# One spectrum for both filter products, a second inverse table, and a reordered start in a Fourier filter with a dense layer behind it

## The chip, the cores and the metric

The kernel runs on one core of a Trainium2 chip. The metric is the device time of one execution in microseconds (us), median of several executions. An execution whose time lies over 1.5% above the fastest of the same kernel is called slow and is left out of every comparison.

## The reference, cut to what matters

```python
def _attn_ref(x, filt_r, filt_i):          # x: 8 x 3008 x 256
    X = np.fft.rfft(x, axis=1)
    F = (filt_r + 1j * filt_i)[None, :, :]
    return np.fft.irfft(X * F, n=x.shape[1], axis=1)

def _moe_ref(x, w_in, w_out):              # 24064 tokens, 256 -> 2048 -> 256
    h = x @ w_in
    return (0.5 * h * (1.0 + erf(h / sqrt(2)))) @ w_out
```

Each of eight batches is filtered in the frequency domain, and the result goes through two dense layers with a Gelu between them.

## The kernel before

The transform of length 3008 is split into 47 x 64. Its four matmul stages are a first transform by table T1, a second by T2, an inverse by T3 and an inverse by T4. Batches 1 to 7 are filtered in slots between the dense matmuls of the batch before. Batch 0 has no dense work to hide behind: it is filtered alone at the start, in the functions named c1 to c4, while the tables are still being made and the filters and weights are still being loaded. The change concerns only this start and three slot numbers.

The stages of batch 0 (cuts are marked with `# ...`):

```python
def dup_filters(self, eng, k0, k):       # rows 0-63 of the filter table to rows 64-127
    for k in range(k0, k0 + k, 2):
        o, i = (self.F[r:r + 64, :, k:k + 2, :].rearrange("p t a b -> p t (a b)") for r in (64, 0))
        eng.tensor_copy(out=o, in_=i)

def c2(self, p):                         # second transform, then the filter product
    w = self.st[0, "p", p] = self.pp.tile([128, 2, 512], BF16, tag="p12", name="p12")
    ps = self.bank("ps_c2", "w")         # two banks: spectrum and i times spectrum
    for t, o in ((0, 1), (1, 0)):
        for i in range(2):
            k = 2 * p + i
            nc.tensor.matmul(ps[:, t, 256 * i:256 * i + 256],
                             lhsT=self.T2[:, k, o:o + 2].rearrange("p a b -> p (a b)"),
                             rhs=self.st[0, "b", k // 4][:, k % 4, :], start=True, stop=True)
    f = self.F[:, :, 2 * p:2 * p + 2, :]
    if p < 11:
        nc.vector.tensor_tensor(out=w, in0=ps, in1=f.rearrange("p t a b -> p t (a b)"), op=ALU.mult)
        return
    # ...

def c3(self, p, np=2):                   # third transform: two separate banks, two evictions
    # ...
    ps = [self.bank("ps_c3", "n") for half in range(2)]
    # ... matmuls with self.T3 for both products ...
    for half in range(2):
        # ...
        self._evac(v[:, :, 8 * p:8 * p + 8 * np], ps[half][:, 0:256 * np].rearrange("c (k n) -> c n k", n=HB),
                   False if p == 11 and half else "act")

def warm_up(self, n):                    # matmuls on a tile of ones, their result is not used
    ps = self.bank("ps_warm", "w")
    for i in range(n):
        self.nc.tensor.matmul(ps[:, i % 2], lhsT=self.ones[:, 0:128], rhs=self.ones, start=True, stop=True)
```

And the order of the start:

```python
m.psum(wide, w=(2, 2), n=(4, 1))         # 2 buffers of 2 banks, 4 of one bank
# ... iotas, first input part, m.warm_up(10), tables, m.load_x(0, 1, 4) ...
for k, n in ((0, 4), (4, 4), (8, 8), (16, 8)):
    m.load_filters(k, n)
m.dup_filters(nc.gpsimd, 4, 4)
m.load_w_in()
m.dup_filters(nc.gpsimd, 8, 8)
for u in range(16):                      # first transform, 4 matmuls and one eviction per u
    m.c1(u // 2, u % 2, act if u < 4 or u % 2 else False)
    if u == 3:
        m.warm_up(3)
        m.table_2_sin(0)
    if u == 7:
        m.table_2_swap(0)
        m.table_2_minus()
        m.warm_up(3)
        m.table_2_sin(1)
    if u == 11:
        m.warm_up(2)
nc.scalar.activation(out=warm, in_=m.p, func=AF.Gelu)
m.warm_up(2)
m.c1t(0, False)
m.c1t(1, act)
m.dup_filters(nc.vector, 0, 4)
# ...
m.dup_filters(nc.gpsimd, 16, 8)
# ... second batch's input, w_out, then c2 and c3 of 12 pairs of frequencies, then c3t and c4
```

## Time and profile before

| | before |
|---|---|
| median time (3 runs) | 773.84 us (773.63 to 774.07) |
| span of the profiled execution | 772.2 us, mean granted clock 1.000 |
| first filter product starts | 16.72 us |
| last filter product ends | 32.02 us |
| first transpose behind it | 32.99 us |
| dense work starts | 40.55 us |
| first matmul of the second layer | 50.92 us |

In the timeline each line has the start, the length, the engine, the source line and the operation with its count, then in brackets the idle time before it and what ended it. The timeline of TensorE, kernel before:

```profile
6.04 1.44 PE L361 MATMUL ps_c<-T1c,x_sb 94*128 94x96 bf16 x16
7.28 0.84 PE L239 MATMUL ps_warm<-ones 128*128 128x512 bf16 x3
9.38 0.84 PE L361 MATMUL ps_c<-T1c,x_sb 94*128 94x96 bf16 x16 [1.25 <-DMA x_sb<-in_x_dram]
```

Sixteen matmuls of the first transform take 1.44 us at 6.04 and 0.84 us at 9.38. Their number and shape are fixed, so this length is a clock that can be read at any place where they stand. In this execution TensorE came to full speed at about 7.3.

### The profile page before, as it was taken

Reading aid. Unit: us, or ns where it says so; the run is one execution under the profiler, and the core shown is the slowest. Engines: PE = TensorE matmul, PEld = TensorE weight load, DVE = VectorE, ACT = ScalarE, POOL = GpSimd, SP = SyncE. Lnnn points to the kernel's source line nnn. Section 1 sums busy time; section 2 is a strip of 40 time slices with the busy share of each in tenths; the row PEclk is TensorE's granted clock in tenths of the full one; section 3 lists DMA queues with packets and bytes.
Section 4 is the critical chain, followed back from the end, with each engine's and each line's share of the span. In section 5 each row is a group of like instructions: output and inputs, shape, how many; then the busy total and the mean of one; then the engine's idle time right before and its main releaser. Section 6 shows DMA issues by size and latency. Waiting matters only on the chain.

```text
span 772.2 us, 15059 instructions
## 1 busy us (share of the span) xinstructions
PE 763.2 (99%) x6066; PEld 528.7 (68%) x6066; DVE 397.3 (51%) x722; ACT 567.4 (73%) x981; POOL 64.9 (8%) x160
## 2 busy tenths in 40 slices
PE   8999999999999999999999999999999999999998
PEld 4847675676776766677777776666776776766666
DVE  7866755464555645457463664637646366411011
ACT  6879955897568975699656996579865798666663
POOL 7801100020000200011000110001100000000000
PEclk9999999999999999999999999999999999999999
DMA  8894745466253661636516464255553422410111
GB/s 138 145 180 124 150 123 129 128 124 151 57 139 107 138 159 41 192 78 122 143 53 181 85 133 123 79 154 95 124 137 81 139 83 69 123 42 28 42 42 55
DMA packets 87398, 85.66 MB, mean 111 GB/s; under 512 B 6752, under 2 KB 77536, under 8 KB 87328
## 3 DMA queue, kind: packets, MB, share of 16 engines
q1 hardware_dynamic: 78816, 68.70, 31.0%
q0 software_dynamic: 8512, 16.00, 14.9%
q8 instruction: 47, 0.77, 0.4%
q14 instruction: 23, 0.19, 0.1%
HBM read 54.00 MB, written 46.66 MB: 130 GB/s over the span
## 4 chain that ended last, share of the span: by engine, by line
PE 94%; DMA 3%; POOL 2%; issue 0%; DVE 0%; POOLq 0%
PE ps_o L488 43%; PE ps_h L461 42%; PE ps_s L345 2%; PE ps_s L320 2%; PE ps_s L295 2%; PE ps_s L272 2%; DMA x_sb<-in_x_dram 2%; POOL F L96 1%; POOL x_sb L82 1%; DMA F<-in_filt_i_dram 1%; POOL F L91 0%; PE ps_e L478 0%; POOL T1s L258 0%; DVE ost L501 0%; POOL T1p L580 0%
## 5 line engine op out<-in xcount | busy, mean ns | idle before, releaser
L464 ACT ACTIVATE g_sb<-ps_h 128x512 bf16<-128x512 f32 x752 | 438.0, 597 | 182.8 <-PE ps_h L461 172.1
L488 PE MATMUL ps_o<-w_out_sb,g_sb 128*128 128x256 bf16 x2992 | 447.5, 273 | 0.0
L461 PE MATMUL ps_h<-y_sb,w_in_sb 128*128 128x512 bf16 (+3 forms) x1600 | 445.8, 366 | 0.7 <-DMA x_sb<-in_x_dram 0.7
L488 PEld LDWEIGHTS <-g_sb 128*128 128x128 bf16 x2992 | 283.9, 98 | 134.3 <-issue 9.9
L461 PEld LDWEIGHTS <-w_in_sb 128*128 128x128 bf16 x1600 | 154.7, 98 | 23.7 <-issue 1.1
L494 DVE COPY ost<-ps_o 128x512 f32<-128x512 f32 x93 | 63.8, 686 | 143.5 <-PE ps_o L488 143.4
L303 DVE TENSOR_TENSOR p<-ps_s,F 128x512 bf16<-128x512 f32 x84 | 58.1, 691 | 105.9 <-ACT p L302 89.5
L249 DVE TENSOR_SCALAR y_sb<-ps_s 128x376 bf16<-128x376 f32 x112 | 60.9, 548 | 80.5 <-PE ps_s L345 80.5
L247 DVE CAST a_sb<-ps_s 128x512 bf16<-128x512 f32 x112 | 69.3, 682 | 27.7 <-PE ps_s L272 27.7
L247 DVE CAST v_sb<-ps_s 128x512 bf16<-128x512 f32 x84 | 57.4, 684 | 2.9 <-PE ps_s L320 2.6
L301 ACT ACTIVATE p<-ps_s 64x512 bf16<-64x512 f32 x84 | 49.9, 594 | 2.1
L302 ACT CAST p<-ps_s 64x512 bf16<-64x512 f32 x84 | 48.5, 577 | 1.0
L345 PEld LDWEIGHTS <-d_sb 96*128 96x128 bf16 x448 | 30.8, 97 | 25.3 <-DMA d_sb<-R 0.2
L101 POOL COPY gate<-p 1x1 bf16<-1x1 bf16 x48 | 8.5, 178 | 470.3 <-DVE p L305 470.3
L305 DVE TENSOR_TENSOR p<-p 128x512 bf16<-128x512 bf16 x84 | 35.7, 425 | 2.9
L345 PE MATMUL ps_s<-T,d_sb 96*128 96x94 bf16 x448 | 36.3, 204 | 0.0
L304 DVE TENSOR_TENSOR p<-p,F 128x512 bf16<-128x512 bf16 x84 | 34.8, 415 | 0.0
L82 POOL DMA_DIRECT2D x_sb<-in_x_dram x64 | 32.7, 512 | 13.0 <-issue 12.5
L320 PE MATMUL ps_s<-p,T 128*128 128x256 bf16 x168 | 32.1, 273 | 0.0
L295 PE MATMUL ps_s<-b_sb,T 128*128 128x256 bf16 x168 | 32.1, 273 | 0.0
L320 PEld LDWEIGHTS <-T 128*128 128x128 bf16 x168 | 16.4, 98 | 20.1 <-DVE p L305 0.5
L295 PEld LDWEIGHTS <-T 128*128 128x128 bf16 x168 | 16.4, 98 | 13.4
(103 smaller groups left out, 189.1 us busy)
## 6 DMA issues: line engine op xcount, KB each, us to landing
out_dram<-ost SPq DMA_DIRECT2D x93, 256.0 KB, 2.3
x_sb<-in_x_dram POOLq DMA_DIRECT2D x64, 188.0 KB, 3.8
R<-a_sb SPq DMA_DIRECT2D x112, 96.0 KB, 2.1
b_sb<-R SPq DMA_DIRECT2D x28, 384.0 KB, 4.3
R<-v_sb SPq DMA_DIRECT2D x42, 256.0 KB, 3.5
d_sb<-R SPq DMA_DIRECT2D x56, 192.0 KB, 4.7
w_in_sb<-in_moe_w_in_dram POOLq DMA_DIRECT2D x2, 512.0 KB, 7.8
w_out_sb<-in_moe_w_out_dram POOLq DMA_DIRECT2D x2, 512.0 KB, 11.3
```

The costliest lines, as they stand in the source:

```text
L247: self.nc.vector.tensor_copy(out=out, in_=in_)
L249: self.nc.vector.tensor_scalar(out=out, in0=in_, scalar1=scale, scalar2=None, op0=ALU.mult)
L295: nc.tensor.matmul(ps[:, 256 * i:256 * i + 256], lhsT=self.T2[:, k, 1:3].rearrange("p a b -> p (a b)"), rhs=self.st[b, "b", k // 6][:, k % ...
L301: nc.scalar.activation(out=p2[0:64], in_=ps[64:128], func=AF.Copy, scale=-1.0)
L302: nc.scalar.copy(out=p2[64:128], in_=ps[0:64])
L303: nc.vector.tensor_tensor(out=p1, in0=ps, in1=f(0), op=ALU.mult)
L320: nc.tensor.matmul(ps[:, 256 * i:256 * i + 256], lhsT=self.T3[:, k].rearrange("p a b -> p (a b)"), rhs=w[:, 256 * i:256 * i + 256], start= ...
L345: nc.tensor.matmul(ps[:, 94 * i:94 * i + 94], lhsT=d[:, (grp % 2) * 4 + i, 128 * half:128 * half + 128], rhs=t4, start=True, stop=True)
L461: nc.tensor.matmul(ps[:, o:o + n], lhsT=self.w_in_sb[:, dc, jc * 128:jc * 128 + 128], rhs=self.ring[:, dc, off:off + n], start=(dc == 0), ...
L464: nc.scalar.activation(out=self.st["g", t][:, jc, :], in_=ps, func=AF.Gelu)
L488: nc.tensor.matmul(ps[:, tile_i % 2, :], lhsT=g[:, jc, tile_i * 128:tile_i * 128 + 128], rhs=self.w_out_sb[:, jc, :], start=(jc == 0), sto ...
L494: nc.vector.tensor_copy(out=ost, in_=ps)
```

## The change

The intent is to spare work in batch 0. The second spectrum (i times the first) is not computed: the imaginary filter multiplies the same spectrum, and the i moves into a second inverse table, T3i, made from T3 by swapping its two columns with a sign. The third transform gets one buffer of two banks (z) and one eviction in place of two. Angles are reduced by an integer shift in place of two float operations. Most filter rows are copied to the upper half of the table by DMA, four copies stay on Pool and one on VectorE. The input is issued earlier, its last part in halves, and the load of the Gelu table moves from the start to the end of the stage. The core of the diff, cuts marked:

```diff
+    def dup_filters_dma(self, k0, k):
+        self.nc.sync.dma_start(out=self.F[64:128, :, k0:k0 + k, :], in_=self.F[0:64, :, k0:k0 + k, :])
 # ... table_2_angle:
-        v.tensor_scalar(out=r, in0=w, scalar1=RND, scalar2=-RND, op0=ALU.add, op1=ALU.add)
-        v.tensor_tensor(out=w, in0=w, in1=r, op=ALU.subtract)
+        ts(out=self.gen[:, 1, k].bitcast(I32), in0=w[:, k].bitcast(I32), scalar1=15, scalar2=None,
+           op0=ALU.logical_shift_left)
+    def table_3_turn(self, q):
+        k = slice(8 * q, 8 * q + 8)
+        for r in range(2):
+            self.nc.vector.tensor_scalar(out=self.T3i[:, k, r, :], in0=self.T3[:, k, 1 - r, :],
+                                         scalar1=self.turn[r], scalar2=None, op0=ALU.mult)
 # ... c2: one spectrum, read twice
-            nc.vector.tensor_tensor(out=w, in0=ps, in1=f.rearrange("p t a b -> p t (a b)"), op=ALU.mult)
+            nc.vector.tensor_tensor(out=w, in0=ps.unsqueeze(1).to_broadcast([128, 2, 512]),
+                                    in1=f.rearrange("p t a b -> p t (a b)"), op=ALU.mult)
 # ... c3: one buffer of two banks, one eviction
-        ps = [self.bank("ps_c3", "n") for half in range(2)]
+        ps = self.bank("ps_c3", "z")
-                                              rhs=self.T3[:, 2 * (p + i) + k].rearrange("p a b -> p (a b)"),
+                                              rhs=(self.T3i if t else self.T3)[:, 2 * (p + i) + k].rearrange("p a b -> p (a b)"),
 # ... the order
-    m.psum(wide, w=(2, 2), n=(4, 1))
+    m.psum(wide, w=(2, 1), n=(4, 1), z=(1, 2))
-    m.warm_up(10)
+    m.warm_up(9)
+    m.dup_filters_dma(2, 2)
+    m.dup_filters_dma(4, 4)
+    m.dup_filters_dma(16, 8)
+    m.table_2_sin(0)
+    for u in range(16):
+        if u == 4:
+            m.table_2_swap(0)
+            m.table_2_angle(g, 1)
+        if u == 8:
+            m.turn_signs(g)
+            m.weights_4(g)
+            m.table_2_sin(1)
+            m.table_2_swap(1)
+        if u == 12:
+            m.table_4(m.T4c, m.T1q, m.wtc)
+        if u in (4, 8, 12):
+            m.warm_up(2)
+        m.c1(u // 2, u % 2, False if u in (1, 3, 5, 7, 8, 9, 12, 14) else act)
 # ... two of three parts of T3i by table_3_turn, the last one by ScalarE
-            s1, n1, r1, s2, n2, r2, s4, n4 = 1, 4, 16, 26, 2.8, 61, 68, 0.72
+            s1, n1, r1, s2, n2, r2, s4, n4 = 0, 4, 15, 25, 2.8, 61, 68, 0.72
```

The matmuls on ones, here called fillers, go from 10 + 3 + 3 + 2 + 2 = 20 to 9 + 2 + 2 + 2 + 1 = 16 (the last one is in a line that the cut leaves out), and they stand at other places.

## The prediction

> **What bounds the kernel now.** I read the page's list of engines first, then its chain that ended last, then the busy time of each engine in seven stretches, and at last the timeline of the first 41 us.
>
> The stretches, each with its length, then the busy us (and count) of PE, PEld, DVE, ACT, POOL, then granted clock, DMA share and GB/s:
>
> ```profile
> 0.00:6.00 6.00, 4.45 (x10) 1.31 (x10) 3.54 (x25) 1.84 (x3) 4.99 (x21) 1.00 0.56 80
> 6.00:14.50 8.50, 6.61 (x76) 4.34 (x76) 7.93 (x15) 6.59 (x14) 5.64 (x11) 1.00 1.02 180
> 14.50:17.00 2.50, 2.13 (x28) 1.92 (x29) 1.75 (x4) 2.48 (x4) 2.50 (x5) 1.00 1.07 148
> 17.00:28.00 11.00, 10.38 (x139) 9.13 (x137) 10.01 (x9) 10.25 (x17) 10.80 (x14) 1.00 1.00 164
> 28.00:40.50 12.50, 10.95 (x188) 9.87 (x185) 10.45 (x16) 9.61 (x23) 8.04 (x17) 1.00 0.76 130
> 40.50:60.00 19.50, 19.41 (x129) 9.99 (x130) 10.44 (x17) 14.15 (x27) 0.00 (x0) 1.00 0.92 202
> 60.00:772.00 712.00, 709.24 (x5507) 492.17 (x5504) 353.22 (x639) 522.51 (x895) 32.95 (x96) 1.00 0.43 107
> ```
>
> From 40.5 us on TensorE is busy 99.6% at full clock. The change leaves that work alone except for three start slots, so 732 of 772 us cannot move much. Only the first 40.5 us, in which batch 0 is filtered alone, are at stake. Their limits, from the timeline (start, length, engine, line, what):
>
> ```profile
> 6.79 0.56 DVE L183 TENSOR_SCALAR gen<-gen 128x768 f32<-128x768 f32 x1
> 7.39 0.96 DVE L184 TENSOR_TENSOR gen<-gen 128x768 f32<-128x768 f32 x1
> ...
> 13.62 0.87 ACT L245 ACTIVATE at_sb<-ps_c 128x384 bf16<-128x384 f32 x2 [0.44 <-PE ps_c L361]
> ...
> 14.51 1.28 ACT L571 ACT_TABLE_LOAD   x1
> ...
> 15.91 0.78 DVE L96 COPY F<-F 64x1024 bf16<-64x1024 bf16 x2
> ...
> 16.72 4.82 DVE L388 TENSOR_TENSOR p<-ps_c,F 128x1024 bf16<-128x1024 f32 x4
> ...
> 21.36 7.93 POOL L96 COPY F<-F 64x1024 bf16<-64x1024 bf16 x8 [0.15 <-DMA F<-in_filt_i_dram]
> ...
> 22.43 6.88 DVE L388 TENSOR_TENSOR p<-ps_c,F 128x1024 bf16<-128x1024 f32 x6 [0.88 <-POOL F L96]
> ...
> 34.87 5.48 ACT L245 ACTIVATE y_sb<-ps_c 128x376 bf16<-128x376 f32 x14 [2.29 <-PE ps_c L438]
> ```
>
> The reader is to see four stages in a row. (1) Until 14.5 the first transform waits for the input: the chain has an input DMA until 12.95, and the last four evictions of at_sb follow it. (2) From 16.72 to 32.02 VectorE multiplies by the filters, product after product, with two gaps (0.88 us here and 0.30 before the product at 29.61; 1.2 in the list of waits), both for Pool's copies of the filter table to its second half. (3) From 32.99 the last transposes and the inverse transform run, evicted by VectorE (8 copies, 5.56 us) and ScalarE (14 evictions, 5.48 us) in balance until 40.40. (4) TensorE starts its dense work at 40.55, after 0.73 us idle; the profile blames the second batch's input, but the last eviction ends at 40.40, so I read it as that eviction.
>
> **What the Trainium skill says.** "VectorE: DVE Perf Modes", section "The perf-mode tier table": tensor_tensor with a PSUM operand runs at 1x, one element per cycle. The trace agrees: 1024 elements took 1.215 us, so reading one spectrum twice by a broadcast view instead of two spectra should save VectorE nothing. The same table gives tensor_scalar on fp32 in SBUF 2x and tensor_tensor 1x; the trace has 0.56 against 0.96 us for 768 elements. No run here shows whether a shift is a 2x case; I take 0.56 us. "ScalarE: Activation LUTs", section "What ACT_TABLE_LOAD costs", gives 1283 ns for a load; the trace has 1.28. "DMA: Bandwidth & Descriptors", section "Issuing engines are not separate DMA queues", says that DMAs of all issuers interleave on the same 16 engines. So filter copies by DMA share with the filter loads; the DMA share is 1.00 to 1.07 from 6 to 28 us, which makes this a real cost.
>
> **The change, part by part.**
>
> Half of the spectrum matmuls go: 24 of 48 of the L383 kind. Four of them take 0.60 us with a tail, about 0.11 us from start to start, so 2.6 us of TensorE. They lie beside VectorE's products, where TensorE had to wait for VectorE anyway. On the path: 0.
>
> The start. The first two input parts are issued before the first iota, so the third, issued at 3.38 now, goes out some 0.5 us earlier, and the last lands at about 12.4 instead of 12.95. After it only two of sixteen evictions are left instead of four, because it comes in halves. But the sine for the big table now stands ahead of all first-transform evictions on ScalarE. The angles of the first half take 384 elements by scalar_tensor_tensor (about 0.6 us), 384 by tensor_scalar (0.36), and one shift (0.56) in place of 1.01 + 0.56 + 0.96; they should end near 6.7 us, and the sine (0.84) near 7.5. From there ScalarE has 8 evictions, 4 swap evictions (0.39 us from start to start each), a second sine (0.84) and T4c (0.36): 5.9 us, plus about 0.4 waiting for the swap matmuls. It ends at 13.8, not 14.49: ScalarE takes over from the input as the limit. Then as now 0.7 us to the first eviction of b_sb, 0.7 for it, and one filter copy on VectorE (0.43) in place of two (0.78). First product at about 15.6 instead of 16.72: **-1.1 us**. The Gelu table load leaves this place for ScalarE's idle 2.29 us before 34.87, where it is hidden; it was not on the path here either.
>
> The products. Now 15.3 us, of which 1.2 wait, so 14.1 bare. Added on VectorE: four small multiplications that build the second inverse table, 512 elements each. The 768-element one of the same type took 0.35, so about 0.25 each, 1.0 us in all, in the middle of the bound engine. Waits left: product 4 needs the filter rows that landed at 21.2 now; with the loads 0.5 us earlier, 384 KB of DMA copies in between, and one Pool copy (1.04 us) after them it starts at about 21.7, where VectorE wants it at about 21.0. I count 0.5. Stage length 14.1 + 1.0 + 0.5 = 15.6: **+0.3 us**.
>
> The step to the tail. The third transform now has one buffer of two banks where it had single banks from a pool of four. Product 10's matmuls wait for the eviction of products 8 and 9 (1.0 us on ScalarE: two of 512 took 1.16 to 1.24), then product 11's for that of product 10. Now 0.97 us pass from the last product to the first L424 transpose; I expect about 1.45: **+0.5 us**.
>
> ScalarE gets two more evictions for the second inverse table's last third, about 1.1 us, ahead of a third-transform eviction, and the single buffer hands the delay on. **+0.2 us**, as the expected part of a risk.
>
> The last part: the second batch's first 8 matmuls (0.56 us) move ahead of the first dense ones, into TensorE's 0.73 us of idle time: **-0.5 us**. Their input is issued near 27 us, behind w_in, and lands near 37.
>
> Sum: -1.1 + 0.3 + 0.5 + 0.2 - 0.5 = -0.6; 773.84 - 0.6 = **773.2 us**.
>
> **The rivals.** First, the filter loads bind: with the copies on the same DMA engines product 4 waits until 22.7, and product 8 for the DMA copy of the last eight rows (512 KB after a landing near 23.5, wanted near 26.5). For it: the DMA share of 1.0 and the 0.15 us wait of Pool at 21.36. Against it: GB/s falls to about 150 in this stretch although the share is full, so the engines may have room. It makes 774 to 775.5. Second, the single buffer binds: per two products it needs about 0.85 us of matmuls, 1.0 of eviction and 0.2 of hand-over, 2.1 against VectorE's 2.4. One backlog of 1.8 us at the three table evictions would be worked off at 0.3 per round only, and since TensorE runs in order, it delays the last spectra too: 774 to 775.5. For it: ScalarE is busy 10.25 of 11 us already. Third, TensorE bound the products after all (10.38 of 11 us busy): then 24 fewer matmuls give up to 2 us more, 771. Against it: VectorE shows no wait on TensorE between products. Fourth, w_in, the second batch's input and w_out all land later than now, and the first second-layer matmul (51.09) waits: up to 1 us.
>
> **Range and chances.** Each term is uncertain by some 0.5 to 1 us and the two binding rivals point up, while a kernel whose splits look this finely chosen may hide waits better than I can see. I take 770.9 to 775.6. Two per cent is 15.5 us, over a third of the whole front: faster 0.02, same 0.965, slower 0.015.
>
> **What would show it.** In the changed timeline: first product near 15.6 (step 1); products of 1.215 us still, four table multiplications near 0.25 us among them, gaps totalling 0.5 (step 2); the first L424-kind transpose 1.45 us after the last product (step 3); the dense work starting near 40.4 with the second batch's matmuls before it (step 4). A third-transform matmul waiting on ScalarE for over a microsecond is rival two; a product waiting on a DMA is rival one. The prediction fails if the first dense matmul comes before 38 or after 43, or if the stretch from there to the end is not 731.5 us within 1.

## The result, and the profile after

| | before | after |
|---|---|---|
| median of fast runs | 773.96 us (773.63 to 774.22, 4 runs) | 784.91 us (782.87 to 785.87, 4 runs) |
| ratio after / before | | 1.0138, 95% interval 1.0117 to 1.0159 |
| first filter product | 16.72 | 20.04 |
| last product ends, stage length | 32.02, 15.30 | 37.84, 17.80 |
| first transpose behind, step | 32.99, 0.97 | 41.27, 3.43 |
| dense work starts, tail | 40.55, 7.56 | 50.44, 9.17 |
| from first second-layer matmul to end of span | 721.28 | 723.38 |

"Dense work starts" is the first matmul behind the last eviction of batch 0: after the change this is one of the second batch's matmuls that were moved ahead, and the first dense one follows at 51.22. A ratio is the mean time of one kernel's fast runs over that of the other's of the same rounds, so it is not quite the ratio of the quoted medians. The change is slower by 1.4%: within the 2% band, which had most of the chance, but 9 us above the range. All rows lose: 3.3 us at the start, 2.5 in the products, 2.5 in the step, 1.6 in the tail, and about 2 after it.

The stretches of the changed kernel that answer to those of the prediction from 14.5 us on (busy us of PE, PEld, DVE, ACT, POOL; granted clock, DMA share, GB/s):

```profile
14.50:17.00 2.50, 2.28 (x25) 1.95 (x25) 1.29 (x3) 1.38 (x4) 2.50 (x6) 1.00 1.11 138
17.00:28.00 11.00, 8.05 (x90) 7.19 (x88) 9.18 (x11) 6.72 (x9) 7.79 (x14) 0.84 0.84 153
28.00:40.50 12.50, 7.84 (x110) 6.66 (x108) 8.96 (x11) 8.64 (x11) 5.04 (x9) 1.00 1.02 193
40.50:60.00 19.50, 17.70 (x187) 11.57 (x190) 15.77 (x26) 13.92 (x30) 0.00 (x0) 0.91 0.69 119
```

TensorE is now idle over a third of the time from 28 to 40.5 (7.84 us busy of 12.5), and no other engine fills that stretch: work waits on work. The granted clock is below 1 in two of these rows, where it was 1.00 in every row before. The timeline of TensorE at the start, changed kernel:

```profile
5.77 1.44 PE L387 MATMUL ps_c<-T1c,x_sb 94*128 94x96 bf16 x16 [0.29 <-DMA x_sb<-in_x_dram]
8.28 0.80 PE L215 MATMUL ps_sw<-T,swap 128*128 128x384 bf16 x2 [1.07 <-ACT at_sb L271]
8.87 1.06 PE L265 MATMUL ps_warm<-ones 128*128 128x512 bf16 x2
9.72 1.49 PE L387 MATMUL ps_c<-T1c,x_sb 94*128 94x96 bf16 x16
12.20 0.80 PE L215 MATMUL ps_sw<-T,swap 128*128 128x384 bf16 x2 [0.99 <-ACT T L208]
```

The group now takes 1.44 to 1.49 us in all four places until 17.4 us, where only the first of the four was slow in the kernel before; only at 17.9 do the times become short. Between the groups stand gaps of 0.29, 1.07 and 0.99 us, the last two while ScalarE, with the sine now ahead of the first transform's evictions, has not yet delivered, and there are fewer fillers than before. Whether this is the cause is for the experiments. The Trainium skill, "TensorE: Matmul & The Clock Gate", section "Part 1: The HAM clock gate", says that the array has 1.2 GHz until it has been busy through a window of about 3.4 us, and 2.4 GHz after. The factor agrees: two fillers take 1.06 us here, and three took 0.84 in the kernel before. A duration is also the safer witness: the granted clock of these stretches reads 1.00, from 0 to 14.5 us and in the first row above.

In the products stage, VectorE's timeline in the changed kernel, and Pool's beside it:

```profile
20.04 1.22 DVE L414 TENSOR_TENSOR p<-ps_c,F 128x1024 bf16<-128x1024 f32 x1
21.19 1.01 DVE L258 TENSOR_SCALAR T3i<-T,turn_r 128x512 bf16<-128x512 bf16 x1
22.11 1.12 DVE L258 TENSOR_SCALAR T3i<-T,turn_i 128x512 bf16<-128x512 bf16 x1
23.16 3.46 DVE L414 TENSOR_TENSOR p<-ps_c,F 128x1024 bf16<-128x1024 f32 x3
...
28.27 0.34 DVE L258 TENSOR_SCALAR T3i<-T,turn_r 128x512 bf16<-128x512 bf16 x1
```

```profile
21.01 4.10 POOL L97 COPY F<-F 64x1024 bf16<-64x1024 bf16 x4 [3.03 <-DMA F<-in_filt_i_dram]
```

The same instruction takes 0.34 us at 28.27, when Pool does not copy, and 1.01 and 1.12 at 21.2 and 22.1, when Pool's copies of 1.03 us each run. The products between them keep their 1.21 to 1.23 us. The Trainium skill, "SBUF — State Buffer", section "Who interferes with whom", says so: a VectorE instruction in a two-port mode and GpSimd lock each other out for a whole instruction, while one with a single SBUF input outside those modes is not touched. The trace agrees with both halves of it.

The chain that ended last in the changed kernel (start, length, what), around the last products:

```profile
36.28 1.07 PE ps_c L431 x16
...
37.37 1.03 ACT vt_sb L271
...
41.27 0.73 PE ps_c3t L451 x8
```

From 34.11 to 40.77 third-transform matmuls and their evictions alternate, 1.07 and 1.03 us (then 0.62 and 0.61), and neither ever overlaps the other, because there is one buffer for both. ScalarE had entered this alternation late: from 30.06 to 33.15 it evicted b_sb, T3 and the last third of T3i one after another. So the step after the last product is 3.43 us. The first 24 transposes behind it then take 2.44 us, and took 1.50 before: in this execution TensorE is slow again from about 41 to 45. It is tempting to blame the idle steps for this, but that is not shown: a1_fill, an experiment below, has the same steps, and its timeline has full speed behind them:

```profile
41.27 2.44 PE L451 MATMUL ps_c3t<-eye,vt_sb 128*128 128x128 bf16 x24 [0.93 <-DVE vt_sb L273]
```

```profile
41.37 1.50 PE L451 MATMUL ps_c3t<-eye,vt_sb 128*128 128x128 bf16 x24 [0.93 <-DVE vt_sb L273]
```

The first of these lines is from the changed kernel, the second from a1_fill.

Last, the filter copies by DMA. The one of 256 KB, from the list of DMA issues up to 45 us (KB, then us from issue to landing):

```profile
F<-F SPq DMA_DIRECT2D x1, 256.0 KB, 7.6
```

It is issued at 16.39 when its rows have landed, and lands at 24.0, behind the later filter loads.

So four suspects lie in one trace: **the clock** (fillers and gaps), **the buffer** (z), **the copies** (DMA) and **the port** (T3i beside Pool). Which of them sets the time cannot be read from it, as each would hide the others. Theory: the first three together make the loss. Rivals: one of them makes it alone, or the new arithmetic itself (T3i and one spectrum) does.

### The profile page after: what moved, and what is told of

Read it like the earlier page. It is cut to its first block, busy times and chain, and to the rows that moved or that the text cites. A ratio compares the mean times of both kernels' runs of the same rounds, so it can differ in the third digit from the quotient of the medians.

```text
span 784.1 us, 14908 instructions
## 1 busy us (share of the span) xinstructions
PE 760.9 (97%) x5937; PEld 531.7 (68%) x6038; DVE 400.0 (51%) x733; ACT 567.7 (72%) x972; POOL 60.1 (8%) x155
## 3 DMA queue, kind: packets, MB, share of 16 engines
q0 software_dynamic: 8640, 16.00, 14.5%
## 4 chain that ended last, share of the span: by engine, by line
PE 91%; DMA 3%; ACT 2%; POOL 1%; issue 1%; DVE 1%; SPq 0%; POOLq 0%
PE ps_o L515 41%; PE ps_h L488 37%; PE ps_s L346 3%; PE ps_s L371 3%; PE ps_s L321 2%; PE ps_s L298 2%; DMA d_sb<-R 1%; PE ps_c L431 1%; DMA x_sb<-in_x_dram 1%; DMA F<-in_filt_r_dram 1%; POOL F L92 1%; ACT y_sb L271 1%; ACT vt_sb L271 1%; DMA b_sb<-R 0%; PE ps_c3t L451 0%
## 5 line engine op out<-in xcount | busy, mean ns | idle before, releaser
L488 PE MATMUL ps_h<-y_sb,w_in_sb 128*128 128x512 bf16 (+3 forms) x1500 | 424.2, 365 | 0.2 <-issue 0.2
```

What stands on the lines that cost most here:

```text
L488: nc.tensor.matmul(ps[:, o:o + n], lhsT=self.w_in_sb[:, dc, jc * 128:jc * 128 + 128], rhs=self.ring[:, dc, off:off + n], start=(dc == 0), ...
```

## The experiments

The fifteen kernels below all gave correct results. "P" is the start of the first product, "E" the end of the last, "T" the first transpose behind it. The kernel before ran beside them (medians 773.91, 774.13, 774.25 and 774.15).

### One part undone at a time

**a1_fill** gives the changed kernel nearly the old number of fillers (19 of 20) near the old places.

```diff
-    m.warm_up(9)
+    m.warm_up(10)
         if u == 4:
+            m.warm_up(3)
             m.table_2_swap(0)
 # ...
             m.table_2_sin(1)
+            m.warm_up(3)
             m.table_2_swap(1)
-        if u in (4, 8, 12):
+        if u == 12:
             m.warm_up(2)
```

> The changed kernel with as many TensorE fillers as the kernel before had, and in like places: 10 at the start, 3 ahead of each of the two swaps (where TensorE waits for ScalarE), 2 at the fourth quarter. Theory A (the clock is the first cause): the changed kernel's TensorE ran at half clock until about 18 us, because one filler less and the sine ahead of the first evictions left it idle too often. Then here 16 first-transform matmuls take 0.84 us instead of 1.49 from the second group on, the first product starts near 16.8 us instead of 20.04, and the time falls by about 3 us to 782. Rival (order alone: ScalarE and VectorE set the pace of that stage whatever the clock): the matmuls get faster or not, but the first product stays at 19 us or later and the time within 1 us of 784.9.

Measured: 784.01 us (782.73 to 785.03), ratio 1.0128. The front did what the clock theory says: P came at 16.87 in place of 20.04. The time did not. VectorE's timeline in this kernel:

```profile
20.12 1.23 DVE L414 TENSOR_TENSOR p<-ps_c,F 128x1024 bf16<-128x1024 f32 x1 [1.50 <-DMA F<-F]
24.32 3.49 DVE L414 TENSOR_TENSOR p<-ps_c,F 128x1024 bf16<-128x1024 f32 x3 [2.97 <-DMA F<-in_filt_i_dram]
```

All that was won at the start is lost in two waits for filter rows, 1.50 and 2.97 us. The late start had hidden them. E is 37.94 and the step again 3.43. The range overlaps that of the change (782.87 to 785.87), so the 0.9 us between the medians is no clear gain.

**a2_pairs** replaces z by two separate banks and two evictions; T3i stays. The pool of single banks becomes six.

```diff
-    m.psum(wide, w=(2, 1), n=(4, 1), z=(1, 2))
+    m.psum(wide, w=(2, 1), n=(6, 1))
-        ps = self.bank("ps_c3", "z")
+        ps = [self.bank("ps_c3", "n") for half in range(2)]
 # ... two evictions, as before the change
```

> The changed kernel with the third transform's PSUM as before: single banks from a pool (now of six), two evictions of 512 instead of one of 1024. Theory B (the single two-bank buffer makes a chain of matmuls, eviction, matmuls): TensorE's waits for the evictions of vt_sb (3.9 us in four waits) go, the last product comes about 1 us earlier, the first transpose of the tail 1.0 to 1.5 us after it instead of 3.4, and since TensorE no longer idles the tail runs at full clock (1.5 instead of 2.4 us for its first 24 transposes): 4 to 5 us off, 780 to 781. Rival (ScalarE's three table evictions are the cause, the buffer only shows it): the step from last product to first transpose stays over 2.5 us and less than 1.5 us is gained.

Measured: 780.31 us (779.36 to 780.92), ratio 1.0080, 4.6 us better than the whole change by the medians. The step is 0.97 again, as in the kernel before, and so is the speed behind it, in the timeline of TensorE:

```profile
37.83 1.50 PE L447 MATMUL ps_c3t<-eye,vt_sb 128*128 128x128 bf16 x24 [0.52 <-DVE vt_sb L273]
```

The expectation counted this speed as a gain of the buffer. That does not follow, since a1, a3 and a4 keep z and its step and show 1.50 here too. P was 19.09: the first transform still had groups of 1.44 and 1.48 us.

**a3_dma88** moves the remaining Pool copies, rows 8 to 15, to DMA, so that Pool never collides with VectorE.

```diff
+    m.dup_filters_dma(8, 8)
     m.dup_filters_dma(16, 8)
 # ...
-    m.dup_filters(nc.gpsimd, 8, 8)
```

> The changed kernel with the filter rows 8 to 15 copied by DMA too, so that GpSimd copies nothing while VectorE builds the second inverse table. Theory C (the two small table multiplications took 1.01 and 1.12 us instead of 0.34 because each waited for a GpSimd copy on a shared port): they take 0.35 us each here, the second product comes 1.5 us earlier, and the time falls by about 1.5 us to 783.4. Rival: the product after it then waits for filter rows that come later by DMA, and nothing is gained (784 to 786).

Measured: 788.61 us (786.68 to 790.39), ratio 1.0192. All T3i multiplications took 0.34 or 0.35 us, so the port theory is confirmed and its 1.4 us are gone. But products waited 4.9 us in two waits for DMA copies, and the kernel became slower by 3.7 us. A Pool copy that costs VectorE something was still cheaper than a DMA copy.

**a4_pool** is the opposite: no copy by DMA, as in the kernel before.

```diff
-    m.dup_filters_dma(2, 2)
-    m.dup_filters_dma(4, 4)
-    m.dup_filters_dma(16, 8)
+    m.dup_filters(nc.gpsimd, 4, 4)
 # ...
-    m.dup_filters(nc.vector, 0, 2)
+    m.dup_filters(nc.vector, 0, 4)
     m.c1t(1, act)
     m.dup_filters(nc.gpsimd, 8, 8)
+    m.dup_filters(nc.gpsimd, 16, 8)
```

> The changed kernel with the filter rows copied to the second half as before: rows 0 to 3 by VectorE, the rest by GpSimd, none by DMA. Theory D (the DMA copies of rows 2 to 7 come at 20 and 24 us because they must wait for the loads and then share the engines with them; GpSimd had rows 4 to 7 by 20.1): no product waits for a filter copy. But alone it should gain little: the first product is at 20 for the clock's sake, and VectorE's two table multiplications still meet GpSimd's copies (1.0 us each) and take the place of the wait. Last product 37.2 to 37.8 instead of 37.84, time 784 to 785. Rival (the DMA copies alone are the cause): last product by 35.5 and the time at 782 or less.

Measured: 786.17 us (783.28 to 786.47), ratio 1.0148: no gain. It lost 1.1 us more than the change, each against the kernel before, but the ranges overlap. P is 21.78, because the two filter copies on VectorE, 0.78 us before, fell beside Pool's copies and took 2.20.

Of these four, only one undoing helped by more than 1 us, and the four answers do not add up to the loss of 11. If the parts hide each other, undoing one shows little.

### Fillers out of the kernel before

**b0_nofill** tests the clock without anything of the change: the kernel before loses its fillers, except for the first ten.

```diff
         if u == 3:
-            m.warm_up(3)
             m.table_2_sin(0)
 # ... the 3, 2 and 2 after it likewise
```

> The kernel before without its ten fillers in the first transform (3 + 3 + 2 + 2); the ten at the start stay. Theory A: TensorE then does not keep, or does not reach, full clock in the input stage; 16 first-transform matmuls take 1.49 us instead of 0.84, and the first product comes 1 to 3 us later than 16.72: 775 to 777. Rival (the clock does not depend on so few fillers): within 0.5 us of 773.9.

Measured: 775.92 us (775.68 to 776.36), ratio 1.0025. From the timeline of TensorE:

```profile
11.32 3.33 PE L361 MATMUL ps_c<-T1c,x_sb 94*128 94x96 bf16 x32
```

Thirty-two of these matmuls take 3.33 us at half clock where 1.6 would do, and P moves from 16.72 to 17.99. So ten matmuls with no result in use are worth 2.0 us here: the clock is real, though smaller than the 3.3 us of the changed kernel.

### All undone together

**a5_three** has the changes of a1, a2 and a4 together. **a6_hybrid** has the same, but leaves the last eight rows to DMA:

```diff
     m.dup_filters(nc.gpsimd, 4, 4)
+    m.dup_filters_dma(16, 8)
 # ...
     m.dup_filters(nc.gpsimd, 8, 8)
-    m.dup_filters(nc.gpsimd, 16, 8)
```

> The changed kernel with the three suspected parts undone at once: as many fillers as before, the third transform's PSUM as before, the filter copies as before. Left of the change: one spectrum and the second inverse table, the shifted angles, the earlier and finer input, the slots. If the three are the causes and only hide each other, then the first product is at 17.2, the last at 33 to 34.5 (two collisions with GpSimd are left), the first transpose 0.97 after it, and the time 774.5 to 776: 9 us of the 11 explained. Rival (something else in the change costs most of it, such as the one spectrum itself): 778 or more.

> As the run before, but rows 16 to 23 by DMA as in the change. By 25 us the loads are over and the copy has the engines to itself, and GpSimd's last copies no longer meet VectorE: the same as the run before or up to 0.7 us faster, 774 to 775.5. If DMA copies are bad wherever they stand, product 8 waits for it and this is 1 us or more slower than the run before.

Measured: a5 779.38 us (778.32 to 780.25), ratio 1.0068; a6 775.20 us (774.73 to 775.88), ratio 1.0018 with interval 1.0001 to 1.0035. So with the fillers, the buffer and most of the copies undone, a6 wins back 9.9 of the 11.0 us, though the three undone one by one gave 0.9, 4.6 and minus 1.1. a5, with every copy undone, wins back only 5.7. In a6, P is 16.35, E 32.45, T 33.41 and dense work starts at 41.08: every milestone within 0.6 us of the kernel before. This holds with one spectrum and T3i still in place.

The two differ in the weights. In a5, Pool is busy with copies until late, so w_in, the second batch and w_out are issued later, and the chain of a5 has a store of a_sb that needed 6.87 us to land beside them. VectorE's next a_sb waited for it and TensorE for that; the first second-layer matmul came at 54.32 in place of 50.92. This is the fourth rival of the prediction, at 3 us.

VectorE's timeline in a6, the remaining collision:

```profile
22.54 0.88 DVE L258 TENSOR_SCALAR T3i<-T,turn_r 128x512 bf16<-128x512 bf16 x1
23.35 1.12 DVE L258 TENSOR_SCALAR T3i<-T,turn_i 128x512 bf16<-128x512 bf16 x1
```

**c1_moved** is a6 with this pair one place later, to leave the collision.

```diff
-            if q == 2:
+            if q == 3:
                 m.table_3_turn(1)
```

> The best so far (fillers, PSUM pairs, filter copies by VectorE, GpSimd and, for rows 16 to 23, DMA) with one move: the second pair of table multiplications goes one round later, after GpSimd's last filter copy (24.3 us). Theory C (they took 0.88 and 1.12 us because GpSimd's copies hold a port that they need): 0.35 each here, last product 1.2 to 1.5 us earlier than 32.45, time about 774.0, at par with the kernel before. Rival (they are long for another reason, such as their place behind a product): still about 1 us each, and the time stays at 775.2.

Measured: fast runs 775.53 to 776.23 us, ratio 1.0018, the same as a6: no gain. Its profiled execution fell in the slow state (798.41 us) and so cannot say where the time went. It gives a hint only: the moved pair took 0.34 and 0.40 us, but a multiplication of the pair before it met Pool instead (1.17), and a product waited 0.60 us for a filter copy by Pool.

### The arithmetic alone

**b1_onespec** puts the one spectrum and T3i, all six parts made by VectorE, into the kernel before, and nothing else.

```diff
-        for t, o in ((0, 1), (1, 0)):
-            for i in range(2):
-                k = 2 * p + i
-                nc.tensor.matmul(ps[:, t, 256 * i:256 * i + 256],
-                                 lhsT=self.T2[:, k, o:o + 2].rearrange("p a b -> p (a b)"),
+        ps = ps[:, 0]
+        for i in range(2):
+            k = 2 * p + i
+            nc.tensor.matmul(ps[:, 256 * i:256 * i + 256], lhsT=self.T2[:, k, 1:3].rearrange("p a b -> p (a b)"),
                                  rhs=self.st[0, "b", k // 4][:, k % 4, :], start=True, stop=True)
 # ... T3i, turn_signs and table_3_turn as in the change; minus plane of T2 not made
```

> The kernel before with one part of the change alone: one spectrum for both filter products and the second inverse table, all of that built on VectorE (six small multiplications). Theory E (VectorE is the bound of the products, TensorE had slack): products stay at 1.2 us, the six add 0.25 to 0.35 us each, or 1 us where GpSimd copies at the same time, so the last product comes 1.5 to 4 us later than 32.02 and the time is 775.3 to 778. Rival (TensorE at 10.4 of 11 us busy was the bound): the products come closer together and the time falls to 772 or 773.

Measured: median 780.78 us, ratio 1.0093, but from 777.44 to 785.84. The products stage is 17.41 us in place of 15.30: the six multiplications took 0.60, 1.12, 0.64, 1.12, 0.34 and 0.34 us, 4.2 in all where 2.0 would do without Pool. Half the spectrum matmuls being gone gives nothing back: products still follow each other every 1.13 us (four in 4.60, as six in 6.88 before). The four times roughly follow the mean granted clock of their runs (777.44 at 1.000, 780.98 at 0.998, 780.57 at 0.996, 785.84 at 0.989), which points to the clock, but only the fastest has a trace. Why the others lost it stays open.

### One part put back at a time

As a6 is nearly as fast as the kernel before, each suspect can be put back alone. **l1_cold** is a6 with the change's fillers, **l2_z** a6 with z, **l3_dma** a6 with the change's copies:

```diff
 # l1_cold, against a6: the five lines of a1_fill undone
 # l2_z, against a6: the lines of a2_pairs undone
 # l3_dma, against a6:
-    m.dup_filters(nc.gpsimd, 4, 4)
+    m.dup_filters_dma(2, 2)
+    m.dup_filters_dma(4, 4)
     m.dup_filters_dma(16, 8)
-    m.dup_filters(nc.vector, 0, 4)
+    m.dup_filters(nc.vector, 0, 2)
```

> PSUM pairs and the mixed filter copies as in the 775.2 run, but the fillers as in the change. Theory A: the input stage runs at half clock again, first product near 19 to 20.5 instead of 16.35; nothing hides it now, so the time is 3 to 4 us above 775.2: 778 to 779.5. Rival: the clock's cost is taken up by other waits, 776 or less.

> Fillers and mixed filter copies as in the 775.2 run, but the single two-bank PSUM buffer of the change. Theory B: the step from the last product to the first transpose is 3.4 us again instead of 0.96, product 10 waits about 1 us for its spectrum; 3 to 4 us above 775.2, 778 to 779.5, more if the tail then runs at half clock. Rival: under 1.5 us.

> Fillers and PSUM pairs as in the 775.2 run, but the filter copies of the change (rows 2 to 7 and 16 to 23 by DMA). Theory D: product 1 waits for rows 2 and 3 until 20, product 2 for rows 4 and 5 until 24; the last product comes near 36.5 instead of 32.45, 4 us above 775.2: 779 to 780. Rival: the waits are covered by the table multiplications, under 1.5 us.

| kernel | median us (range) | ratio | above before | above a6's 1.1 | P | E - P | T - E |
|---|---|---|---|---|---|---|---|
| a6_hybrid | 775.20 (774.73 to 775.88) | 1.0018 | 1.1 | | 16.35 | 16.10 | 0.96 |
| l1_cold | 780.60 (778.92 to 781.32) | 1.0077 | 6.4 | 5.3 | 20.63 | 17.61 | 0.97 |
| l2_z | 780.88 (779.53 to 781.88) | 1.0082 | 6.6 | 5.6 | 17.45 | 17.68 | 3.43 |
| l3_dma | 779.20 (777.81 to 780.12) | 1.0066 | 5.0 | 3.9 | 16.08 | 19.33 | 0.98 |

Each suspect alone costs 3.9 to 5.6 us, and each mostly in its own column: the clock at P, the buffer in the stage and the step, the copies in the stage. The columns are not clean. Of the 4.3 us that l1 loses at P, 1.1 are two filter copies on VectorE that now fall beside Pool's (1.84 us, 0.76 in a6), and in its stage, longer by 1.5 us, the first pair of T3i multiplications now meets Pool too (1.21 and 1.12 us) and two waits of 0.60 and 0.34 us come in. In l1 the last group of the first transform is as slow as in the whole change, from TensorE's timeline:

```profile
14.78 1.49 PE L387 MATMUL ps_c<-T1c,x_sb 94*128 94x96 bf16 x16
```

In l2 and in l3, from VectorE's timeline of each:

```profile
32.71 1.23 DVE L414 TENSOR_TENSOR p<-ps_c,F 128x1024 bf16<-128x1024 f32 x1 [1.39 <-PE ps_c L410]
```

```profile
23.43 3.48 DVE L414 TENSOR_TENSOR p<-ps_c,F 128x1024 bf16<-128x1024 f32 x3 [3.13 <-DMA F<-in_filt_i_dram]
```

In l2 a product waits 1.39 us because its spectrum matmuls follow third-transform matmuls in TensorE's timeline, and those wait before the occupied buffer, and then the step is 3.43, the same as in the change. A part of l2's loss, the 1.1 us at P, probably belongs to the banks rather than to the order: z also takes two single banks from the first transform, which has six in a6, and in l2 TensorE waits 0.96 us at 8.30 for an eviction of at_sb that it need not wait for in a6. In l3 two waits for filter rows, 1.24 and 3.13, are the loss; 1.3 us of it come back, since no T3i multiplication meets Pool there any more.

The sum of the three is 14.7 us, and the change has 9.9 above a6. They overlap: a late start (clock) hides the late filter rows (DMA). This settles the theory against the rival of one cause alone. Against the other rival stands a6, which has the new arithmetic and is 1.1 us above the kernel before; where the arithmetic did cost more, in b1, four of its multiplications lay beside Pool's copies.

### The wished-for gains alone

**s0_slots** has only the new slots of the second batch in the kernel before. **s1_start** adds the change's issue order of the input. **s2_start_dma** adds to this the DMA copy of the last eight rows.

```diff
 # s0
-            s1, n1, r1, s2, n2, r2, s4, n4 = 1, 4, 16, 26, 2.8, 61, 68, 0.72
+            s1, n1, r1, s2, n2, r2, s4, n4 = 0, 4, 15, 25, 2.8, 61, 68, 0.72
 # s1, also
+    m.load_x(0, 0, 8)
     m.p = m.iota(g, "p", [128, 1], [[0, 1]], cm=1)
 # ... input parts between the iotas, as in the change
+    m.load_x(0, 24, 8, step=4)
 # s2, also
+    m.dup_filters_dma(16, 8)
-    m.dup_filters(nc.gpsimd, 16, 8)
```

> The kernel before with the second batch's three start slots one earlier, as in the change, and nothing else. The prediction's step: its first 8 matmuls fill TensorE's 0.73 us of waiting for the last eviction, so 0.5 us less, 773.4. Rival: they wait for the same PSUM banks as the dense work does and come no earlier; 773.9 unchanged.

> The kernel before with the change's input order (two parts before the first iota, last part in halves) and its slots; two spectra, fillers, PSUM and GpSimd copies of the kernel before. If the start was worth what the prediction said: last input part near 12, first product at 16.0 to 16.4 instead of 16.72, filter loads 0.5 us earlier, last product near 31.5, time 772.9 to 773.4. Rival: ScalarE and VectorE then bind, first product within 0.2 us of 16.72, and no gain but that of the slots.

> As s1_start, with filter rows 16 to 23 copied by DMA. The 0.30 us wait of the last products for GpSimd goes, and the later loads are issued 4 us earlier: 0.3 us less than s1_start, 772.6 to 773.1. Rival: the copy shares the engines with the weight load (issued near 20 us) and the ninth product waits for it: 0.5 us or more above s1_start.

Measured: s0 773.93 us (773.44 to 774.42), ratio 0.9993; s1 774.15 (773.90 to 775.61), ratio 1.0000; both intervals include 1. s2 780.96 (780.23 to 781.88), ratio 1.0087. In s0 the second batch's matmuls do stand first, but they wait 0.6 us for the last eviction of y_sb too, so there is no idle time to fill. In s1 the last input part lands at about 13.3, before at about 13.0: issuing the first part earlier does not bring the last one earlier, and P is 16.61. In s2 VectorE's timeline has:

```profile
32.99 3.55 DVE L390 TENSOR_TENSOR p<-ps_c,F 128x1024 bf16<-128x1024 f32 x3 [5.81 <-DMA F<-F]
```

This kernel, like the one before the change, issues w_in amid the products, at about 20.5, and the copy shares the engines with it: 5.81 us of waiting. In the changed kernel, where w_in is issued behind Pool's copies (at 26.0), the same copy of 512 KB took 4.4 us, and no wait of a product for it appears. So where the weights are issued decides what this copy costs.

No version was measurably faster than the kernel before.

## Why the prediction was wrong, point by point

The band was right, the sum wrong by nearly 12 us. One cause, the clock, is missing from it; the terms of the start and of the slots failed, and those of the products and of the step had the right mechanism and the wrong size. Both signs of failure that the prediction named came true: the first dense matmul came at 51.22, after its limit of 43, and the stretch from there to the end of the span was 732.9 us, outside its 731.5 within 1.

**The start, "-1.1 us": failed.** Measured +3.3. The sum of ScalarE's operations held: in a6, ScalarE runs from 7.09 to 14.04 almost without a gap, and the prediction said 13.8. What was missing is the clock. The prediction counted fillers nowhere and treated the length of TensorE's groups as fixed. With gaps of 0.29, 1.07 and 0.99 us each group took 1.44 to 1.49 us instead of 0.84, ScalarE waited for them in turn, and P came at 20.04; a1 moved it to 16.87 by fillers alone, and l1 from 16.35 to 20.63 by taking them away (1.1 of it by filter copies that then met Pool's). Nor was the expected 15.6 reached with the clock mended (16.08 was the best, in l3): the input landed only about 0.2 us earlier (about 12.8 after, 13.0 before), where the prediction had 0.55.

**The products, "+0.3 us": mechanisms right, size wrong.** Measured +2.5. The products kept their 1.21 us, as predicted from the tier table. The T3i multiplications are 0.34 us undisturbed, not 0.25, and 1.01 and 1.12 beside Pool, so 2.8 us in all where the sum had 1.0: the two-port lock was not considered, though Pool's copies were in the plan. The waits for filter rows, counted at 0.5, are the first rival. In the changed kernel they are hidden by the late start, and 4.5 us when this is mended (a1). The estimate took a landing time for the loads and gave the copies little beyond it; the copies are issued only after that landing, then took 5.4, 7.6 and 4.4 us. Issuing is not the cost: the section of the DMA page cited in the prediction says that all issuers share the same engines, and s2 shows the size of it.

**The step, "+0.5 us", and ScalarE's table evictions, "+0.2 us": mechanism right, size wrong.** Measured +2.5 at the step and up to 0.9 before it. The second rival described just this, a backlog that is worked off at 0.3 us per round. But it was priced as if enough rounds were left to work it off. It comes with the last table third at 30 to 33 us, and then matmuls and eviction alternate at 1.07 + 1.03 us, which is hardly faster than VectorE's 2.4 per two products, until the end. l2 gives z 5.6 us in all.

**The tail, 0 us: failed.** Measured +1.6. TensorE ran slowly here once more (24 transposes in 2.44 us, 1.50 before). The cause stays open: a1, a3, a4 and l2 have the same step of about 3.4 us before the tail, yet their 24 transposes took 1.50 us and their tail 7.6 us, as in the kernel before. So this row may belong to the one profiled execution, and not to the change.

**The slots, "-0.5 us": failed.** s0 gives a ratio of 0.9993. The 0.73 us of idle time before the dense work was itself an eviction's end, as the prediction had read it, and matmuls moved ahead wait for the same.

**The matmuls spared, 0 us: right.** b1 shows no gain from them, and the third rival (TensorE bound the products) falls. **The hidden Gelu load: right.** It stands at 40.78, where ScalarE has nothing else to do.

**Left open.** From the first second-layer matmul on, the variants differ by up to 2.3 us (721.1 to 723.4) with waits of TensorE on d_sb and b_sb loads of 0.4 to 0.9 us, at different places from run to run; no experiment isolates them. The last 1.1 us of a6 and the spread of b1 are not settled either, nor why the fillers hold the clock in one execution and not quite in another: l1 reached full speed for one group at 9.10 and lost it again at 11.12, and a2, a3 and a4, with the change's fillers, had their first group at 0.84 us and the next one at 1.44 to 1.49. That fillers decide over the time of the start is shown (b0, a1, l1); by which rule of gaps and busy time they do it is not.

## What to carry to other kernels

Before moving anything in a sparsely occupied start, measure TensorE's clock by the length of a group that never changes, and treat matmuls without a result as part of the schedule. When several parts of a change each produce a wait, undoing one of them may show nothing, since the next wait takes its place: undo all, then put each back alone. A pair of buffers that becomes a single one, or a copy that moves to DMA, should be priced by the last round before the stage ends, where no slack is left to work off a backlog.

## What the Trainium skill lacked or had wrong

- "TensorE: Matmul & The Clock Gate", section "Part 1: The HAM clock gate", gives a warm-up budget of about 3.4 us, all after it at full speed. Here, with nine fillers from 1.46 us and then gaps of 0.29, 1.07 and 0.99 us, TensorE stayed slow until about 17.9 in the profiled execution of the change, some 16 us. Gaps alone do not decide it: full speed was lost behind a gap of 1.18 us in l1 and kept over 1.23 in a6, 1.62 in s0 and 1.81 in b1. The page's section "A second HAM failure mode: psum-queue depth-cycling" names short idle times between groups, but no length; these are some.
- The same page, section "Part 4: PE-mode transpose", says that the full clock does not engage for transposes. Here eight transposes by nc.tensor.transpose took 0.61 us in fast stretches and 1.05 to 1.06 in slow ones, so these had the full speed where the matmuls around them had it.
- The same page, section "Seeing it yourself", warns that clock events in a trace are unreliable, and names one way, a low reading that stays for over 50 us. Here it was the other way: the granted clock read 1.00 from 6 to 14.5 us, where groups took 1.44 and 1.49 us in place of 0.84. Later in the same trace it did agree with the durations: 0.58 from 41 to 45 us, where the transposes were slow.
- "VectorE: DVE Perf Modes", section "The perf-mode tier table", has no integer row. The page's conditions for the modes name operands and shapes, and none that would tell whether a shift is among the operations enabled for 2x. 768 int32 elements took 0.56 and 0.67 us, much as a float tensor_scalar with 0.56 and 0.60.
- "ScalarE: Activation LUTs", section "What ACT_TABLE_LOAD costs", adds a drain of 1.38 us to each load. Here the load takes 1.28 us and the next instruction starts 0.02 us behind it (40.78 and 42.08), with no gap ahead of it either.
- "DMA: Bandwidth & Descriptors" has no time for a single copy from one part of SBUF to another beside other loads. Here 128, 256 and 512 KB took 5.4, 7.6 and 4.4 us from issue to landing, the last one with little beside it.
